# Attention and dense layers on one core: two interleaved streams in a hand-set order, x kept in SBUF, DMA transposes, head pairs on array tiles

## The chip, the cores and the metric

The kernel runs on one core of a Trainium2 chip. The metric is device time in microseconds (us) of that core. Executions of the kernel before spread over 2%.

Engines are named as in the profile: PE is TensorE's matmul, PEld its weight load, DVE VectorE, ACT ScalarE, POOL GpSimd, SP SyncE (here only an issuer of DMAs).

## The reference

Eight batches of twelve heads, 448 tokens, 64 features per head; then two dense layers over the 8 x 448 = 3584 tokens. Cut to what matters:

```python
q_n = q / (norm(q) + 1e-06);  k_n = k / (norm(k) + 1e-06)
attn = softmax(q_n @ k_n.T / tau)             # tau = 0.1
x = (attn @ v)  ->  [3584 tokens, 12 * 64 = 768]
h = x @ w_in                                  # 768 -> 2048
out = maximum(0.01 * h, h) @ w_out            # 2048 -> 768
```

## The kernel before

Batches of attention and chunks of 512 tokens of dense work are written one after the other, and a tile scheduler interleaves them. Per head:

```python
# weights are loaded first, then q, k, v of each batch; rows of 64 f32 = 256 bytes
nc.gpsimd.dma_start(out=w_in_sb, in_=w_in_r);  nc.gpsimd.dma_start(out=w_out_sb, in_=w_out_r)
...
for h in range(H):
    for t in range(NK):                       # 4 tiles of 112 tokens
        nc.vector.tensor_scalar_mul(out=q_hn[:, t, :], in0=q_bf[:, h, t, :],
                                    scalar1=qni[:, h, t : t + 1])
    for t in range(NK):                       # 8 PE transposes into PSUM
        nc.tensor.matmul(out=pqk[:, 0, t, :], lhsT=q_hn[:, t, :], rhs=id128[:PK, :PK], is_transpose=True, ...)
        nc.tensor.matmul(out=pqk[:, 1, t, :], lhsT=k_bf[:, h, t, :], rhs=id128[:PK, :PK], is_transpose=True, ...)
    nc.vector.tensor_copy(out=qkT, in_=pqk)
    for ki in range(NK):
        nc.tensor.matmul(out=sc, lhsT=kT[:, ki, :], rhs=qTf, start=True, stop=True)
        nc.scalar.activation(out=pe[:, ki, :], in_=sc, func=Exp, scale=kni[:, h, ki : ki + 1])
    for ki in range(NK):                      # a 65th column of ones in v gives the sums
        nc.tensor.matmul(out=po, lhsT=v_bf[:PK, h, ki, :], rhs=pe[:, ki, :], ...)
    nc.vector.reciprocal(rsi, po[D : D + 1, :])              # 1 x 448
    nc.gpsimd.partition_broadcast(out_ap=rsb, in_ap=rsi)
    nc.vector.tensor_mul(obf, po[:D, :], rsb)
    nc.sync.dma_start(out=xT[h * D : (h + 1) * D, b * S : (b + 1) * S], in_=obf)   # x to DRAM
```

A dense chunk loads its 512 columns of x back from DRAM, does 16 x 6 matmuls of 512 columns with a leaky ReLU on ACT, and 4 x 2 x 16 matmuls of 512 or 256 columns with a copy on ACT.

## Time and profile before

| before | value |
|---|---|
| time, median of the first 3 runs | 810.55 us (807.48 to 821.59) |
| first matmul | 52.4 us |
| 52 to 240 us: weighing matmuls (attn @ v) done, of 384 | 100, that is 25 of 96 heads |
| granted clock in most of that stretch | 0.50 to 0.59 |
| PE busy from 440 us on | 91 to 99% per stretch of 40 us |

The page's first part (busy time per engine) and three rows of its second (the span in 40 slices of 20.3 us, a digit being tenths):

```profile
PE 664.0 (82%) x3054; PEld 281.4 (35%) x3104; DVE 543.4 (67%) x714; ACT 375.0 (46%) x616; POOL 126.0 (16%) x128
PE   0036775977479988899889999799999999999996
PEclk9999655555559979999598999899999999999999
DMA  9999009305980099009190099207970012001201
```

There are three stages in these digits. For two slices PE does nothing while the DMA engines are full. Then PE is partly busy at half clock. From the middle on it is nearly always busy at full clock.

The costliest groups (line, engine, operation, tiles, shapes, count | busy us, mean ns | idle before, and what ended it):

```profile
L132 ACT ACTIVATE pe<-sc,kni 112x448 bf16<-112x448 f32 x384 | 243.0, 633 | 236.9 <-PE sc L129 235.7
L144 DVE RECIPROCAL rsi<-po 1x448 f32<-1x448 f32 x96 | 282.8, 2949 | 98.7 <-PE po L139 97.8
L112 PE MATMUL tp<-id_58,q_hn 112*64 112x112 bf16 x384 | 66.6, 243 | 68.6 <-DVE q_hn L106 66.3
```

The reciprocal works on one row and costs 2.95 us per head. PE's waits, longest first (total us, times, longest):

```profile
PE tp L112 <- DVE q_hn L106: 66.3, 3, 52.4
PE sc L129 <- ACT pe L132: 31.0, 56, 2.7
```

The 52.4 us are the start. How matmuls follow one another is read from the timeline by differences of starts, since a matmul's end is modelled (start, us, what):

```profile
651.73 0.39 PE L129 MATMUL sc<-qkT 64*112 64x448 bf16 x1
652.05 0.38 PE L139 MATMUL po<-pe,v_bf 112*65 112x448 bf16 x1
652.26 0.81 PE L191 MATMUL po_4942<-w_out_sb,hT 128*128 128x512 bf16 x3
```

A score matmul of 448 columns occupies the array for 0.32 us here, a weighing one for 0.21.

### The profile page before, as it was taken

The numbers are of one execution on the slowest core, as the hardware profiler recorded it, in microseconds if no ns is written. First come the engines' busy times: TensorE is split into PE (matmuls) and PEld (weight loads), VectorE is DVE, ScalarE is ACT, GpSimd is POOL, SyncE is SP. The second block draws the span as 40 slices with busy tenths as digits, with TensorE's granted clock in tenths as the row PEclk, the third lists the DMA queues.
The fourth block names the chain that finished last, engine by engine and source line by source line (L and its number), as shares of the span: only waits on it lengthen the run. The fifth ranks groups of instructions, "written<-read, shape, count | busy, mean of one in ns | idle before, by whom it ended". The sixth has DMA issues, their size and how long they took to land.

```text
span 811.7 us, 8243 instructions
## 1 busy us (share of the span) xinstructions
PE 664.0 (82%) x3054; PEld 281.4 (35%) x3104; DVE 543.4 (67%) x714; ACT 375.0 (46%) x616; POOL 126.0 (16%) x128
## 2 busy tenths in 40 slices
PE   0036775977479988899889999799999999999996
PEld 0012321322123334333343335333443344334543
DVE  0087877767867877689486887789978874775000
ACT  0034434433436653566436664566465643663231
POOL 3120113112301131013110132012201110111000
PEclk9999655555559979999598999899999999999999
DMA  9999009305980099009190099207970012001201
GB/s 172 192 126 29 12 10 99 17 11 44 57 58 12 10 96 104 37 13 68 35 118 25 9 74 88 80 9 55 80 112 12 9 36 96 13 9 36 93 19 59
DMA packets 149496, 45.36 MB, mean 56 GB/s; under 512 B 131536, under 2 KB 145104, under 8 KB 149456
## 3 DMA queue, kind: packets, MB, share of 16 engines
q0 software_dynamic: 132256, 22.81, 53.7%
q1 hardware_dynamic: 17200, 22.03, 8.8%
q8 instruction: 24, 0.39, 0.2%
q14 instruction: 16, 0.13, 0.1%
HBM read 51.12 MB, written 16.52 MB: 83 GB/s over the span
## 4 chain that ended last, share of the span: by engine, by line
PE 64%; ACT 9%; issue 9%; DVE 8%; DMA 7%; POOL 2%; another core or an unknown queue 1%; POOLq 0%; ACTq 0%; SPq 0%; DVEq 0%
PE pm L166 19%; PE sc L129 16%; PE po L139 12%; ACT pe L132 5%; PE tp L112 4%; DMA k_bf<-in_k_dram 4%; PE tp L117 3%; DVE rsi L144 2%; DMA xTc<-xT_bridge 2%; DMA xT_bridge<-obf 1%; DVE q_hn L106 1%; ACT L94 1%; DVE kni L88 1%; DVE qni L88 1%; ACT osb L197 1%
## 5 line engine op out<-in xcount | busy, mean ns | idle before, releaser
L132 ACT ACTIVATE pe<-sc,kni 112x448 bf16<-112x448 f32 x384 | 243.0, 633 | 236.9 <-PE sc L129 235.7
L144 DVE RECIPROCAL rsi<-po 1x448 f32<-1x448 f32 x96 | 282.8, 2949 | 98.7 <-PE po L139 97.8
L129 PE MATMUL sc<-qkT 64*112 64x448 bf16 x384 | 171.4, 446 | 41.7 <-ACT pe L132 31.0
L166 PE MATMUL pm<-xTc,w_in_sb 128*128 128x512 bf16 x641 | 181.4, 388 | 7.5 <-DMA xTc<-xT_bridge 4.1
L139 PE MATMUL po<-pe,v_bf 112*65 112x448 bf16 x384 | 157.1, 431 | 9.3 <-ACT pe L132 8.7
L146 POOL PARTITION_BROADCAST rsb<-rsi x96 | 75.4, 787 | 525.1 <-DVE rsi L144 474.2
L112 PE MATMUL tp<-id_58,q_hn 112*64 112x112 bf16 x384 | 66.6, 243 | 68.6 <-DVE q_hn L106 66.3
L191 PEld LDWEIGHTS <-hT 128*128 128x128 bf16 x896 | 87.1, 101 | 81.1 <-issue 31.6
L129 PEld LDWEIGHTS <-qkT 64*112 64x112 bf16 x384 | 51.3, 136 | 167.4 <-issue 148.8
L166 PEld LDWEIGHTS <-w_in_sb 128*128 128x128 bf16 x672 | 64.2, 103 | 56.9 <-issue 11.0
L112 PEld LDWEIGHTS <-q_hn 112*64 112x64 bf16 x384 | 43.1, 122 | 109.2 <-DVE q_hn L106 71.1
L173 ACT ACTIVATE hT<-pm 128x512 bf16<-128x512 f32 x112 | 66.6, 594 | 25.4 <-PE pm L166 23.1
L139 PEld LDWEIGHTS <-v_bf 112*65 112x65 bf16 x384 | 43.6, 120 | 100.3 <-issue 85.8
L106 DVE TENSOR_SCALAR q_hn<-q_bf,qni 112x64 bf16<-112x64 bf16 x384 | 70.9, 268 | 10.0 <-PE tp L112 6.1
L122 DVE COPY qkT<-tp 64x896 bf16<-64x896 bf16 x96 | 59.1, 615 | 25.3 <-PE tp L117 23.4
L148 DVE TENSOR_TENSOR obf<-po,rsb 64x448 bf16<-64x448 f32 x96 | 58.9, 616 | 21.0 <-POOL rsb L146 20.0
L117 PE MATMUL tp<-id_58,k_bf 112*64 112x112 bf16 x384 | 66.1, 239 | 0.0
L117 PEld LDWEIGHTS <-k_bf 112*64 112x64 bf16 x384 | 45.6, 125 | 11.2 <-issue 11.1
L87 DVE TENSOR_TENSOR norm_sq<-q_bf 112x3072 bf16<-112x3072 bf16 x8 | 14.3, 1786 | 42.2 <-DMA q_bf<-in_q_dram 38.9
L88 DVE TENSOR_REDUCE qni<-norm_sq 112x48 f32<-112x3072 bf16 x8 | 26.6, 3329 | 2.8 <-issue 2.8
L88 DVE TENSOR_REDUCE kni<-norm_sq 112x48 f32<-112x3072 bf16 x8 | 26.7, 3341 | 0.2
L77 POOL DMA_DIRECT2D v_bf<-in_v_dram x8 | 16.0, 1999 | 61.8 <-PE po L139 29.6
(133 smaller groups left out, 297.2 us busy)
## 6 DMA issues: line engine op xcount, KB each, us to landing
out_dram<-osb SPq DMA_DIRECT2D x28, 384.0 KB, 2.3
q_bf<-in_q_dram POOLq DMA_DIRECT2D x8, 672.0 KB, 8.7
k_bf<-in_k_dram POOLq DMA_DIRECT2D x8, 672.0 KB, 9.9
v_bf<-in_v_dram POOLq DMA_DIRECT2D x8, 672.0 KB, 11.0
xT_bridge<-obf SPq DMA_DIRECT2D x96, 56.0 KB, 1.9
xTc<-xT_bridge SPq DMA_DIRECT2D x7, 768.0 KB, 5.0
w_in_sb<-in_moe_w_in_dram POOLq DMA_DIRECT2D x1, 3072.0 KB, 18.6
w_out_sb<-in_moe_w_out_dram POOLq DMA_DIRECT2D x1, 3072.0 KB, 21.9
```

The source lines that it names most:

```text
L88: nc.vector.tensor_reduce(ni_tile, sq, axis=mybir.AxisListType.X, op=mybir.AluOpType.add)
L106: nc.vector.tensor_scalar_mul(out=q_hn[:, t, :], in0=q_bf[:, h, t, :], scalar1=qni[:, h, t : t + 1],)
L112: nc.tensor.matmul(out=pqk[:, 0, t, :], lhsT=q_hn[:, t, :], rhs=id128[:PK, :PK], is_transpose=True, start=(t == 0), stop=False,)
L117: nc.tensor.matmul(out=pqk[:, 1, t, :], lhsT=k_bf[:, h, t, :], rhs=id128[:PK, :PK], is_transpose=True, start=False, stop=(t == NK - 1),)
L129: nc.tensor.matmul(out=sc, lhsT=kT[:, ki, :], rhs=qTf, start=True, stop=True,)
L132: nc.scalar.activation(out=pe[:, ki, :], in_=sc, func=mybir.ActivationFunctionType.Exp, scale=kni[:, h, ki : ki + 1],)
L139: nc.tensor.matmul(out=po, lhsT=v_bf[:PK, h, ki, :], rhs=pe[:, ki, :], start=(ki == 0), stop=(ki == NK - 1),)
L144: nc.vector.reciprocal(rsi, po[D : D + 1, :])
L146: nc.gpsimd.partition_broadcast(out_ap=rsb, in_ap=rsi)
L166: nc.tensor.matmul(out=pm, lhsT=w_in_sb[:, kt, m * 128 : (m + 1) * 128], rhs=xTc[:, kt, :], start=(kt == 0), stop=(kt == KT_DM - 1),)
L173: nc.scalar.activation(out=hT[:, m, :], in_=pm, func=mybir.ActivationFunctionType.Prelu, alpha=0.01,)
L191: nc.tensor.matmul(out=po2[:, :osz], lhsT=hT[:, m, ts * PT : (ts + 1) * PT], rhs=w_out_sb[:, m, ofs : ofs + osz], start=(m == 0), stop=(m ...
```

## The change

The intent: pair the heads, so that two matmuls of 64 rows (row tiles) or 64 columns (column tiles) lie side by side on the array; take the transposes, the DRAM round trip of x and half the reciprocals off the engines; and give PE an instruction order in which dense matmuls fill the time in which attention waits. The new file is a rewrite. Its core, with cuts marked:

```diff
-    q_r = q.rearrange("b h (t p) d -> b h p t d", p=PK)          # 256-byte rows
+    view = "b h (p t) d -> b p h t d"                            # rows of 4 tokens: 1 KB
+    ctx.enter_context(tc.manual_schedule())                      # program order on each engine
+    nc.scalar.preload_act_table_set("natural_log_exp_and_others")
 ...
+    def turn(b, what):                                           # 16 DMA transposes in all
+        nc.sync.dma_start_transpose(out=xt[...], in_=xn.rearrange("p t h d -> p (t h d)"))
-            nc.tensor.matmul(... is_transpose=True ...)          # 768 of them
-            nc.vector.tensor_copy(out=qkT, in_=pqk)
 ...
+    def scores(b, p, half):                                      # two heads on row tiles
+        for ki in (2 * half, 2 * half + 1):
+            for a in range(2):
+                r = slice(64 * a, 64 * a + 64)
+                nc.tensor.matmul(out=sc[:, a, :S], lhsT=kT[r, o : o + 128], rhs=q4[r, :, p, :], ...)
+            nc.scalar.activation(out=pe[:, ki], in_=sc[:PK, :, :S], func=ACTF.Exp, scale=inv_tau)
+    def weigh(b, p):                                             # two heads on column tiles
+        for dst, ones_ in ((sm, True), (po, False)):
+            for ki in range(NT):
+                for a in range(2):
+                    nc.tensor.matmul(out=dst[64 * a : 64 * a + 64, :],
+                        lhsT=ones[:PK, :] if ones_ else vb[:, 2 * p + a, ki, :],
+                        rhs=pe[:, ki, a, :], start=(ki == 0), stop=(ki == NT - 1))
+        nc.vector.reciprocal(rs, sm)                             # 128 x 448, once per pair
+        nc.vector.tensor_mul(st["x", b][:, p, :], po, rs)        # x stays in SBUF
-            nc.gpsimd.partition_broadcast(out_ap=rsb, in_ap=rsi)
-            nc.sync.dma_start(out=xT[...], in_=obf)
 ...
+    def fill(us):                                  # dense work, on an estimated clock
+        end = clock[0] + us
+        while at[0] < len(dense) and clock[0] < end:
+            work, took, b = dense[at[0]]           # layer 1: 1.13 us, layer 2: 2.6 us
+            if done.get(b, 1e9) + 6.0 > clock[0]:  # x of batch b not there yet
+                break
+            work(); clock[0] += took; at[0] += 1
 ...
+    for what in "qkv":
+        load(0, what)
+    nc.gpsimd.dma_start(out=w_in_sb, ...);  nc.gpsimd.dma_start(out=w_out_sb, ...)
+    ... norms, scaling and transposes of batch 0 ...
+    for what in "qkv":
+        load(1, what)
+    for b in range(B):
+        for p in range(HP):                        # 6 head pairs
+            for half in range(2):
+                scores(b, p, half)
+                if half == 1: weigh(the pair before)
+                prepare(b + 1, 2 * p + half)       # norms, scaling, transposes, loads, by step
+                fill(3.0)
```

A half-pair is the work of one call of `scores`: a head pair against two of the four key tiles. `prepare` spreads the next batch over the half-pairs: sums of q at step 0, root of q and sums of k at step 1, root of k at step 2, scaling on POOL from step 3, transposes at steps 4 and 5, the loads after next at steps 6 and 11.

## The prediction

> **What bounds it now.** Three stages. (1) Start: by the waits view PE's first matmul comes at 52.4 us; the two weight loads were issued ahead of q and k, and the loads' 256-byte rows keep the DMA 90% busy to 40 us. (2) About 52 to 240 us: little or no dense work, granted clock 0.50 (stretch table), PE about 75% busy at that clock, and the chain alternates score matmul, 0.64 us exp, 2.95 us reciprocal, broadcast. (3) From about 440 to 812 us PE is 91 to 99% busy per stretch at clock 0.91 to 1.0: PE-bound. Page: PE 664, DVE 543, ACT 375, POOL 126 us of 812.
>
> **Removed.** 768 PE transposes (started 0.05 us apart warm: about 38 us of PE), 96 PSUM copies (59 us DVE), 384 small scalings (71 us DVE), half of the reciprocals (96 to 48 of 2.95 us: 141 us DVE), 75 us of broadcasts, about 40 us of ACT table loads, the DRAM round trip of x, and three quarters of the q/k/v packets (rows become 1 KB).
>
> **Added.** A ones-matmul for the sums; 16 DMA transposes of 688 KB; scaling on POOL (84 calls, about 1.2 us each, estimate); mode changes on the array: in the trace a 448-column score matmul between full-array ones takes 0.32 us start to start, against 0.19 to 0.21.
>
> **Costs after (estimates from those spacings: 448 columns 0.19 us, 384 columns 0.16).** Dense: 768 x 0.19 + 896 x 0.16 = 290 us, cannot shrink. Scores: 384 matmuls in row-tile pairs, 192 x 0.19 = 37. Sums and values: 768 in column-tile pairs, 384 x 0.19 = 73; unpaired it would be 146. The Trainium skill, "TensorE: Matmul & The Clock Gate", Part 3, reports concurrent tiles at 3.07x for four; no run here shows pairs yet. Mode changes, about 0.2 us each around 96 score and 48 weighing groups: 30. PE total about 430. ACT: exp of 896 columns about 0.91 us x 192 = 175, Prelu 69, copies 27, norms 9: 280. DVE: 142 + 30 + 82 + 11 = 265. So PE binds wherever dense work is interleaved, ACT or DVE elsewhere.
>
> **Time by stage (order of the built kernel).** Start until the first score matmul: 33 us (loads, two norms at 5.1 us, scaling, transposes beside the weight load). The first 19 half-pairs have no dense work, at half clock, about 2.65 us each: 50. Then 59 half-pairs hold 235 us of dense work plus 1.45 us of attention each: 320. Another 18 in batches 3, 5, 7 have none, limited by DVE (10 us of norm sums there) and ACT: 45. After the last attention: 17 us of batch 6 and 39 of batch 7, plus hand-over and last store: 60. Sum 508; imperfect pairing and stalls add about 20: **528 us**, ratio about 0.65. Range **485 to 600**. Chances: faster 0.98, same 0.01, slower 0.01.
>
> **What would show it.** Two score matmuls of a pair starting within 0.05 us, and 16 weighing matmuls in 1.5 to 2.0 us (not 3.0). First matmul at 28 to 40 us. One ACT table load. Exp about 0.91 us. Clock near 0.5 for the first 80 to 90 us and about 1.0 in the dense stretches. Weights, x and transposes never topping PE's waits after the start. A dense-only tail near 56 us. POOL under half busy.
>
> **What would make it wrong.** Column-tile matmuls with different moving operands not overlapping (+70 us). Slow weight loads on column tiles. DMA transposes much slower than 10 us each, above all beside the weight load at the start (+10 to 20). The clock halving again in the attention-only stretches of batches 3, 5, 7 (+10 to 30). POOL's scaling several times dearer than estimated, so that a batch waits for its transposes.

## The result, and the profile after

The changed kernel takes 555.61 us (median of 4 runs, 554.02 to 557.2), against 809.01 us before (4 runs of the same rounds, 804.96 to 821.59). The ratio is 0.689, 95% interval 0.685 to 0.693. A ratio here is the mean time of one kernel's runs over that of the other's of the same rounds, so it is not quite the ratio of the medians. Executions over 1.5% slower than the fastest of the same kernel are left out of the means.

The same lines of the page, after (slices of 13.8 us now):

```profile
PE 446.2 (81%) x2816; PEld 216.5 (39%) x2816; DVE 265.8 (48%) x163; ACT 260.0 (47%) x409; POOL 118.3 (21%) x131
PE   0000285589999999499999996799999997999996
PEclk9999999789999999679999999799999999999999
DMA  9999829448149423392449025290560110002013
```

PE now starts in the fifth slice, at 62.7 us, and from the ninth on the row has three dips, in the 17th, the 25th and 26th, and the 34th. The groups that answer those of before:

```profile
L135 ACT ACTIVATE pe<-sc 112x896 bf16<-112x896 f32 x192 | 163.2, 918 | 60.9 <-PE sc L131 60.9
L153 DVE RECIPROCAL rs<-sm 128x448 f32<-128x448 f32 x48 | 141.8, 2953 | 180.9 <-PE sm L146 180.9
L103 POOL TENSOR_TENSOR q_n<-q_bf,q_ni 112x512 bf16<-112x512 bf16 x42 | 42.3, 1038 | 80.9 <-DVE q_ni L99 80.9
```

A reciprocal of 128 rows costs what one of 1 row did (2.953 against 2.949 us), so halving the count halved the cost. PE's waits:

```profile
PE sc L131 <- DMA kT<-k_n: 64.6, 2, 62.7
PE sc L131 <- ACT pe L135: 37.7, 46, 5.4
```

The first matmul waits 62.7 us, and for the k transpose. SP's timeline shows the transposes of batches 0 to 2 (start, time during which SP was issuing it, what):

```profile
24.98 10.41 SPq L114 DMA_TRANSPOSE qT<-q_n  x1
35.45 18.77 SPq L114 DMA_TRANSPOSE kT<-k_n  x1
74.64 3.36 SPq L114 DMA_TRANSPOSE qT<-q_n  x1
81.43 3.74 SPq L114 DMA_TRANSPOSE kT<-k_n  x1
113.94 3.21 SPq L114 DMA_TRANSPOSE qT<-q_n  x1
```

The first two take three to six times as long to issue as the later ones. And the pairs, in a dense stretch of the same timeline:

```profile
159.34 0.55 PE L131 MATMUL sc<-qT,kT 64*128 64x448 bf16 x4
159.83 0.95 PE L146 MATMUL sm<-pe,ones 112*64 112x448 bf16 x8
160.61 0.92 PE L146 MATMUL po<-pe,v_bf 112*64 112x448 bf16 x8
```

Four score matmuls occupy 0.49 us, eight weighing ones 0.78: one 448-column matmul per 0.12 and 0.10 us, where it was 0.32 and 0.21. The single records show the pairs: the score matmuls start at 159.344 and 159.348 us, then at 159.544 and 159.548, and the weighing ones too in twos, 3 to 4 ns apart.

The dips, as stretches (the columns are the length, and each engine's busy time in it; only rows of interest):

```profile
120.00:217.00 97.00, 97.00 (x628) 48.14 (x626) 47.33 (x29) 53.29 (x86) 16.85 (x20) 1.00 0.52 83
217.00:239.00 22.00, 13.56 (x75) 4.94 (x74) 18.24 (x13) 11.02 (x17) 14.08 (x17) 0.66 0.46 77
338.00:358.00 20.00, 11.18 (x75) 4.32 (x73) 17.34 (x13) 11.00 (x17) 12.10 (x14) 0.83 0.51 84
456.00:469.00 13.00, 9.03 (x77) 3.96 (x76) 11.23 (x7) 10.15 (x13) 0.00 (x0) 1.00 0.09 27
```

Where dense work is interleaved (120 to 217 us) PE is busy all the time. In batches 3, 5 and 7 there is a stretch without it, in which DVE, at 83 to 87%, is the busiest engine, and the granted clock falls in two of the three.

Where the time came from, by stage, in the two profiled executions (spans of 811.7 and 553.5 us, 258 apart; the medians are 253 apart):

| stage | before | after |
|---|---|---|
| to the first matmul | 52.4 us | 62.7 us |
| attention with next to no dense work | 52 to 240: 188 us for 25 heads (7.5 each) | 62.7 to 119: 56 us for 19 heads (3.0 each) |
| the rest, mostly PE-bound | 572 us | 434 us |

So the start lost 10 us, and the two other stages gave 132 and 138 us. They don't hold the same share of the work before and after, which is why the second row has the time per head too.

### The profile page after: what moved, and what is told of

Same layout as the page of the kernel before. It is cut to its first block, busy times and chain, and to the rows that moved or that the text cites. A ratio compares the mean times of both kernels' runs of the same rounds, so it can differ in the third digit from the quotient of the medians.

```text
span 553.5 us, 6672 instructions
## 1 busy us (share of the span) xinstructions
PE 446.2 (81%) x2816; PEld 216.5 (39%) x2816; DVE 265.8 (48%) x163; ACT 260.0 (47%) x409; POOL 118.3 (21%) x131
## 4 chain that ended last, share of the span: by engine, by line
PE 73%; DVE 9%; DMA 8%; ACT 5%; SPq 2%; POOL 1%; issue 1%; ACTq 0%; DVEq 0%; POOLq 0%
PE mm L164 27%; PE mm L180 27%; PE sm L146 7%; DMA kT<-k_n 7%; PE sc L131 6%; PE po L146 6%; ACT pe L135 5%; DVE k_ni L87 2%; DVE rs L153 2%; SPq L114 2%; DMA q_bf<-in_q_dram 1%; DVE k_n L86 1%; DVE q_ni L87 1%; POOL k_n L103 1%; DVE q_n L86 1%
## 5 line engine op out<-in xcount | busy, mean ns | idle before, releaser
L153 DVE RECIPROCAL rs<-sm 128x448 f32<-128x448 f32 x48 | 141.8, 2953 | 180.9 <-PE sm L146 180.9
L135 ACT ACTIVATE pe<-sc 112x896 bf16<-112x896 f32 x192 | 163.2, 918 | 60.9 <-PE sc L131 60.9
L164 PE MATMUL mm<-xT,w_in_sb 128*128 128x448 bf16 x768 | 153.9, 355 | 0.0
L180 PE MATMUL mm<-w_out_sb,hT 128*128 128x384 bf16 x896 | 150.1, 326 | 0.0
L131 PE MATMUL sc<-qT,kT 64*128 64x448 bf16 x384 | 62.7, 383 | 102.4 <-DMA kT<-k_n 64.6
L168 ACT ACTIVATE hT<-mm 128x448 bf16<-128x448 f32 x128 | 69.8, 545 | 76.4 <-PE mm L164 76.4
L103 POOL TENSOR_TENSOR q_n<-q_bf,q_ni 112x512 bf16<-112x512 bf16 x42 | 42.3, 1038 | 80.9 <-DVE q_ni L99 80.9
L103 POOL TENSOR_TENSOR k_n<-k_bf,k_ni 112x512 bf16<-112x512 bf16 (+1 forms) x43 | 50.6, 1209 | 22.8 <-DVE k_ni L99 22.8
L146 PE MATMUL sm<-pe,ones 112*64 112x448 bf16 x384 | 51.5, 395 | 0.2 <-DVE rs L153 0.2
L146 PE MATMUL po<-pe,v_bf 112*64 112x448 bf16 x384 | 50.0, 387 | 0.0
## 6 DMA issues: line engine op xcount, KB each, us to landing
w_in_sb<-in_moe_w_in_dram POOLq DMA_DIRECT2D x1, 3072.0 KB, 26.3
```

Of the source, the lines that this page charges most:

```text
L103: eng.tensor_tensor(out=xn[:, :, h0:h1, :].rearrange("p t h d -> p h t d"), in0=x[:, h0:h1], in1=ni[:, h0:h1].unsqueeze(3).to_broadcast([P ...
L131: nc.tensor.matmul(out=sc[:, a, :S], lhsT=kT[r, o : o + 128], rhs=q4[r, :, p, :], start=True, stop=True,)
L135: nc.scalar.activation(out=pe[:, ki], in_=sc[:PK, :, :S], func=ACTF.Exp, scale=inv_tau)
L146: nc.tensor.matmul(out=dst[64 * a : 64 * a + 64, :], lhsT=ones[:PK, :] if ones_ else vb[:, 2 * p + a, ki, :], rhs=pe[:, ki, a, :], start=( ...
L153: nc.vector.reciprocal(rs, sm)
L164: nc.tensor.matmul(out=pm[:, :S], lhsT=w_in_sb[:, kt, m * 128 : (m + 1) * 128], rhs=xT[:, kt, :], start=(kt == 0), stop=(kt == KT - 1),)
```

## The experiments

Two questions were open. Which parts of the change earn the time? And why is it 28 us more than the 528 us forecast, when the forecast's costs per instruction were met? The theory for the second: the first transposes share the DMA engines with 12.6 MB of weights (the f32 bytes read), and the attention-only stretches are held up by DVE's norm sums. The rivals: the first transposes are slow by themselves; and ScalarE's order, not DVE, makes the stretches slow.

All edits are to the changed kernel. Times are medians of 4 runs (e14: 6):

| run | time, us | ratio to before |
|---|---|---|
| changed kernel | 555.6 | 0.689 |
| e1 weights after the first transposes | 555.1 | 0.688 |
| e2 batch 1's loads after them too | 554.9 | 0.688 |
| e3 loops of the weighing swapped | 556.5 | 0.690 |
| e4 root of k later | 556.5 | 0.691 |
| e3b full-array weighing (wrong result) | 612.2 | 0.759 |
| e5 scheduler's order | 555.6 | 0.689 |
| e6 dense work spread | 526.9 | 0.653 |
| e9 weights in gaps | 559.7 | 0.693 |
| e12 loads reordered | 535.3 | 0.662 |
| e14 e12 and e6 together | 506.1 | 0.626 |
| e8 x through DRAM | 555.2 | 0.688 |
| e15 full-array scores (wrong result) | 566.9 | 0.702 |

The changed kernel wasn't run again in the rounds of the experiments, and the rounds used different chips in part. Differences of a few us from its 555.6 are therefore not read as gains or losses.

### Do the pairs earn it? e3, e3b, e15

e3 was meant to take the column pairs apart by order alone:

```diff
-            for ki in range(NT):
-                for a in range(2):
+            for a in range(2):
+                for ki in range(NT):
                     nc.tensor.matmul(out=dst[64 * a : 64 * a + 64, :], ...
```

> The changed kernel with the two loops of the weighing swapped: the four key tiles of one head run one after the other, then those of the other head, so that neighbouring matmuls share a column tile. Same matmuls, same data, same number. Theory (neighbouring matmuls on different column tiles run at the same time): eight of them take about 1.5 us in place of 0.78, PE gains 48 x 1.5 = 72 us of work, of which the dense stretches (37 of 48 pairs) show all: time 600 to 630 us. Rival (the array would overlap them anyway, or the pairs are not what makes them quick): 550 to 565 us.

It measured 556.5 us: nothing. The trace shows that the experiment missed its aim, for the weighing is as fast as before:

```profile
163.29 0.96 PE L146 MATMUL sm<-pe,ones 112*64 112x448 bf16 x8
164.08 0.95 PE L146 MATMUL po<-pe,v_bf 112*64 112x448 bf16 x8
```

Within the eight of the sums, single records still start in twos, 13 ns apart, about every 190 ns. The program as written has four matmuls in a row on one column tile. The records don't name the tile, and they don't show whether the built program kept that order, so that the second four overtook the first is an inference. For the time, the order among the eight made no difference here.

e3b takes the pairs away for real. The result is wrong:

```diff
-  out=dst[64 * a : 64 * a + 64, :], lhsT=ones[:PK, :64] or vb[:, 2 * p + a, ki, :]       # 64 columns
+  out=dst,                          lhsT=ones[:PK, :128] or 128 columns of vb            # 128 columns
```

> A wrong result on purpose: the 16 weighing matmuls of a head pair keep their number, moving operands and columns, but each uses 128 weight columns and writes all 128 rows of sums or values, so that no two can sit side by side on the array. Since the swap of loops changed nothing (two matmuls still started 13 ns apart every 189 ns, although program order put four on one column tile in a row), this is the real removal of the pairs. If the pairs halve the weighing: eight matmuls in 1.5 us instead of 0.78, 48 x 1.45 = 70 us more PE work, time 605 to 630 us. If they do not, 550 to 562 us.

```profile
172.93 0.55 PE L131 MATMUL sc<-qT,kT 64*128 64x448 bf16 x4
173.41 1.69 PE L146 MATMUL sm<-pe,ones 112*128 112x448 bf16 x8
174.93 1.30 PE L146 MATMUL po<-pe,v_bf 112*128 112x448 bf16 x6
```

Eight matmuls now occupy 1.52 us instead of 0.78, and the time is 612.2 us. The column pairs are worth 56.6 us.

e15 does the same to the scores: `lhsT=kT[:, ...]` and `rhs=q4[:, ...]` over all 128 rows.

> A wrong result on purpose: the score matmuls keep their number and columns, but each uses all 128 rows (both heads of the pair at once), so that no two can run side by side on row tiles. If the row pairs halve the scores as the column pairs halved the weighing: four matmuls in about 0.8 us instead of 0.48, 96 groups x 0.35 = 33 us more PE work, a part of it hidden in the attention-only stretches, so 575 to 592 us. If the row pairs earn nothing (their saving lost in changing the array's mode around each group): 550 to 562 us.

```profile
165.99 0.92 PE L131 MATMUL sc<-qT,kT 128*128 128x448 bf16 x4
166.74 3.57 PE L164 MATMUL mm<-xT,w_in_sb 128*128 128x448 bf16 x18
```

A group of four takes 0.75 us, not 0.8, against 0.49 paired. Time 566.9 us: 11.3 us more, between what the two expectations named. The saving is 0.26 us a group, less than half of 0.75; that a paired group changes the array's mode and a full-array one in a dense stretch does not would account for it (see the list below), but no run isolates it. Over the roughly 59 groups in dense stretches that would be 15 us. A part of it came back: in this run batch 0's weighing reached full pace by 69.8 us, in the changed kernel only by 80.5 (the first record of a granted clock begins at 67.6 and 77.4 us). A busier PE getting its clock sooner would fit this, but wasn't tested.

### Does the order, or x in SBUF, earn it? e5, e8

e5 deletes one line, `ctx.enter_context(tc.manual_schedule())`, and lets the scheduler reorder.

> The changed kernel with the hand-set order given up: the line that keeps program order on each engine is removed and the tile scheduler may reorder. In the built program the order of the dense stretches is the same, but the attention-only stretches differ: single layer-1 matmuls and copies are pulled in among the scores. If the hand-set order carries part of the gain: 565 to 590 us. If the structure carries it and not the order: 548 to 562 us.

555.6 us: the hand-set order, beyond the order in which the program is written, earns nothing that these runs can show. The waits move (PE waits for exp 12.6 us instead of 37.7, but 14.4 us for DVE's multiply and 7.1 for ScalarE's copy), and the time stays.

e8 sends x through DRAM again:

```diff
-        nc.vector.tensor_mul(st["x", b][:, p, :], po, rs)
+        nc.vector.tensor_mul(xo, po, rs)
+        nc.sync.dma_start(out=xTd[p * 128 : (p + 1) * 128, b * S : (b + 1) * S], in_=xo)
+        if p == HP - 1:  nc.sync.dma_start(out=st["x", b], in_=xTd[:, batch b] ...)
```

> One part of the change undone: x goes to DRAM by one 448-column write per head pair and comes back by one load per batch, as before the change. In the changed kernel batch 0's x is complete at 102.1 us and first used at 119.0 us, so 17 us of slack against about 7 us for the write (1.9 us) and the load (5.0 us) measured in the kernel before. If the round trip lies within the slack: 552 to 562 us, x in SBUF earns nothing by itself. If it is on the chain: 575 to 620 us, with PE waiting for the load of x once per batch.

555.2 us. The round trip lies within the slack that the order of the dense work leaves; keeping x in SBUF earns nothing measurable here.

### The start: e1, e2, e9, e12

e1 holds the weights back. A copy of two columns that reads the landed transpose and writes into the weight tile makes the load wait, without a race:

```diff
-    nc.gpsimd.dma_start(out=w_in_sb, ...); nc.gpsimd.dma_start(out=w_out_sb, ...)    # before batch 0's norms
 ... norms, transposes of batch 0, load(1, ...)
+    nc.gpsimd.tensor_copy(out=w_in_sb[:, 0, 0:2], in_=st["kT", 0][:, 0:2])
+    nc.gpsimd.dma_start(out=w_in_sb, ...); nc.gpsimd.dma_start(out=w_out_sb, ...)
```

> The changed kernel, but the two weight loads are issued only after the first k transpose has landed (a two-column copy that reads that transpose's result and writes into the weight tile goes ahead of the load); the loads of batch 1 stay where they are. Theory A (the first two transposes take 10.4 us of issue and 27.2 us to landing because they share the 16 DMA engines with 12.6 MB of weights): first score matmul at 38 to 46 us instead of 62.7, time 530 to 540 us. Rival B (the first transposes are slow by themselves, for instance because they are the first): first score matmul stays at 58 to 64 us, time stays 550 to 560 us. Rival C (the start shrinks, but the weights then come too late for the first dense work): first matmul early, and a wait for the weights of 5 us or more appears before the first layer-1 matmul.

e2 moves the copy above batch 1's loads as well.

> As the run before, and the q, k and v loads of batch 1 are held back as well, so that nothing else is loading while q and k of batch 0 are transposed. Theory A: both transposes at their undisturbed pace (about 5 us from issue to landing), first score matmul at 35 to 38 us, 3 to 8 us earlier than in the run before; time 525 to 537 us. If the loads of batch 1 do not matter, the first matmul is where it was in the run before. If holding them back makes batch 1's transposes late, a wait for the transpose of 3 us or more appears at the start of batch 1.

Both confirm the mechanism and neither gains: 555.1 and 554.9 us. PE's longest wait in e1:

```profile
PE sc L131 <- DMA kT<-k_n: 62.0, 2, 39.6
```

The 62.0 us are two waits, of 39.6 us for batch 0's transpose and of 22.4 for batch 1's. SP's timeline in e1 has both pairs of transposes:

```profile
24.86 3.38 SPq L114 DMA_TRANSPOSE qT<-q_n  x1
30.05 3.81 SPq L114 DMA_TRANSPOSE kT<-k_n  x1
57.00 16.31 SPq L114 DMA_TRANSPOSE qT<-q_n  x1
73.40 12.90 SPq L114 DMA_TRANSPOSE kT<-k_n  x1
```

Without the weights beside them, batch 0's transposes are issued as quickly as any, so they are not slow by being the first. The first matmul came at 39.6 us, with batch 1's loads beside the k transpose, and at 35.2 us in e2, with nothing beside it. But now batch 1's transposes meet the weights and take 16.3 and 12.9 us to issue. Batch 1's first score came at 92.9 and 95.1 us, where it had been 92.5. What was gained at the first batch was paid at the second.

The DMA packets say why. A transpose is 2688 packets of 256 bytes, 168 on each of 16 engines. Alone, one takes 18 ns (median). The layer-2 weights come in packets of 1536 bytes at 134 ns, q and k in packets of 512 bytes at 60 ns. The Trainium skill, "DMA: Bandwidth & Descriptors", section "Queues, rings and completion order", states that each DMA engine goes round-robin between its queues, a packet at a time (a packet in the page's sense can hold several of the rows that the profile counts as packets). If each transpose packet waits for one of the others, the estimate is 168 x 134 ns = 22.5 us beside the weights, and 168 x (60 + 18) ns = 13 us beside q and k. Measured from issue to landing: 26.3 us for the changed kernel's first q transpose, whose packets ran beside the weights nearly all the way, 11.0 us for its second k transpose, beside the loads of q and k for the most part, and 5.1 us alone (e2). The first k transpose took 27.2 us because it stood behind the q transpose in its queue: it landed 11.4 us after it, with batch 1's loads beside it. The sizes fit, and the packet records of the trace show the alternation, one for one in number: from 36.0 to 47.2 us 1257 packets of transposes and 1254 of the layer-2 weights started, from 54 to 60 us 1442 of transposes and 1425 of batch 1's loads.

e9 puts the layer-1 weights after batch 1's loads, and the layer-2 weights after batch 1's k transpose.

> Runs e1 and e2 moved the first matmul to 39.6 and 35.2 us, but batch 1's k transpose then landed at 92.9 and 95.1 us (92.5 before): it had met the weights instead. Here the layer-1 weights go out after batch 0's transposes and batch 1's loads, and the layer-2 weights only after batch 1's k transpose has landed. Theory F (one 256-byte transpose packet waits for a large weight packet at each turn, so a transpose must have the queue engines to itself): first matmul at 34 to 37 us, batch 1's first score at 69 to 76 us, time 528 to 540 us. Rival G (the volume of loads alone sets when batch 1 can start): batch 1's first score at 85 us or later, time above 545 us.

Both of batch 1's transposes ran nearly alone (6.9 and 6.6 us from issue to landing) and the second landed at 72.6 us, as theory F has it. Yet the time was 559.7 us, for the gain went a third way:

```profile
95.79 1.76 DVE L86 TENSOR_TENSOR q_n<-q_bf 112x3072 bf16<-112x3072 bf16 x1 [19.59 <-DMA q_bf<-in_q_dram]
102.44 0.56 PE L131 MATMUL sc<-qT,kT 64*128 64x448 bf16 x2 [24.55 <-ACT pe L135]
```

Batch 2's q load had queued behind the layer-2 weights and landed at 95.8 us. The root of its sums stands in ScalarE's program order ahead of batch 1's exps, so the exps waited for a load that they don't need. The waits view blames "ACT pe" for 24.6 us; the cause is a DMA two steps back.

e12 keeps e9's place for the layer-1 weights, issues batch 2's q and k loads ahead of the layer-2 weights, and takes up batch 2's preparation four half-pairs later (cut):

```diff
+        if b == 2:
+            step -= 4
 ...
         elif step == 6 and b + 1 < B:
+            if b == 1: nc.gpsimd.tensor_copy(out=w_out_sb[:, 0, 0:2], in_=st["kT", 1][:, 0:2])
             load(b + 1, "q"); load(b + 1, "k")
+            if b == 1: nc.gpsimd.dma_start(out=w_out_sb, ...)
```

> Run e9 brought batch 1's k transpose in at 72.7 us, but batch 2's q load then queued behind the layer-2 weights, landed at 95.8 us, and the root of batch 2's q sums, ahead of the exps in ScalarE's order, held PE for 24.6 us. Here batch 2's q and k loads go ahead of the layer-2 weights, and batch 2's norms, scaling and transposes are taken up four half-pairs later in batch 1. If this chain of late loads is the whole reason why e1, e2 and e9 gained nothing: no wait of PE above 5 us after the first matmul except for batch 1's k transpose (at 72 to 75 us), first layer-1 matmul at 95 to 103 us in place of 119.0, time 530 to 542 us. If the time comes back once more, above 548 us, and the wait that takes it is to be named.

```profile
PE sc L131 <- ACT pe L135: 46.7, 46, 9.9
PE sc L131 <- DMA kT<-k_n: 35.0, 1, 35.0
```

535.3 us, with the first layer-1 matmul at 95.7 us instead of 119.0. The gain of 20 us is kept. One expectation failed: a wait of 9.9 us for exp is left, up to 49.5 us. It is of the kind that e9 showed: batch 1's q, whose load was held back, gets its sums at 48.0 us, and the root of them stands ahead of batch 0's exps.

### The attention-only stretches: e4, e6

e4 moves only the root of k, which stands ahead of the exps in ScalarE's order, from step 2 to step 5 (its inverse, scaling and transpose go with it).

> The changed kernel with the square root of k's sums moved three steps later in ScalarE's order (its inverse, scaling and transpose move with it). Theory (the exps of the next pairs stand behind a root that waits for 8 us of VectorE work, 5.4 us of PE idle in batch 3, 4.1 us in batch 1, the same in batch 5): these waits shrink to under 1.5 us, PE's waits for exp fall from 37.7 us to 20 to 27, time 538 to 550 us. Rival (VectorE itself is the limit there, so that the wait moves to the sums matmul behind the reciprocal): time 551 to 558 us and a new wait of PE for the reciprocal of 8 us or more in sum.

```profile
PE sc L131 <- ACT pe L135: 23.2, 40, 0.9
PE sm L146 <- DVE rs L153: 14.6, 3, 5.0
```

556.5 us. The waits for exp fell from 37.7 to 23.2 us, and 14.6 us of waits for DVE's reciprocal took their place. In batches 3 and 5 a wait of 5.4 us for exp became one of 4.8 us for the reciprocal. (In batch 1 the k transpose, moved with the root, kept PE waiting for 8.2 us where it had been 1.9.) The rival is right: DVE is the limit in these stretches. It has 3.6 us per head pair and another 10.2 us of norm sums at the stretch's beginning.

e6 gives DVE time instead. The dense work is handed out by a running account, so that no stretch is without it:

```diff
     def fill(us):
-        end = clock[0] + us
+        owed[0] += us                       # what a half-pair overshoots is taken off the next
+        end = clock[0] + owed[0]
 ...
-            fill(3.0)
+            fill(3.05)                      # and a third buffer for x
```

In the old form every half-pair got its 3.0 us afresh, so two layer-2 groups (5.2 us) counted as one allotment, and the stock of dense work ran out in every second batch.

> The changed kernel with the dense work handed out by a running account (3.05 us per half-pair, the overshoot carried to the next half-pair) instead of afresh per half-pair, and a third buffer for x. The batches 3, 5 and 7 then have no stretch without dense work. Theory D (in these stretches VectorE's norm sums hold up attention, because no PE work is there to cover them, and the clock halves): PE's waits for exp fall from 37.7 to about 15 us, time 525 to 538 us. Rival E (what is gained there comes back as ScalarE or VectorE waits in the dense stretches): 548 to 558 us.

The row "PE" of e6's page, and PE's longest wait for ScalarE:

```profile
PE   0000186759999999999999999999999999999996
```

```profile
PE sc L131 <- ACT pe L135: 15.7, 25, 4.2
```

526.9 us, 28.7 less, and the dips of the row "PE" are gone. The third buffer for x came with it, and its own share wasn't measured.

### Both together: e14

e14 is e12 with e6's account, and with the margin between a batch's attention and its dense work cut from 6.0 to 3.0 on the kernel's own clock.

> The reordered loads of the run above, the dense work spread by a running account (run e6), and the margin between a batch's attention and its first dense work cut from 6 to 3 on the kernel's own clock. If the two gains are in different places and add up: 526.9 - 20 and a few us for the earlier dense work, 495 to 510 us, PE idle after its first dense matmul below 10 us in sum. If the start's gain is lost again: 520 to 530 us. This is the version meant to beat both kernels.

The row "PE" of e14's page, and PE's two longest waits:

```profile
PE   0011868599989999999999999999899999999996
```

```profile
PE sc L131 <- DMA kT<-k_n: 35.0, 1, 35.0
PE sc L131 <- ACT pe L135: 19.4, 21, 9.8
```

506.1 us (6 runs, 503.78 to 507.96), correct, ratio 0.626 to before. It beats both kernels. The gains of e12 (20.3 us) and e6 (28.7 us) add up to 49.0, and 49.5 came, with the cut of the margin, whose own share was not measured. PE's waits after its first dense matmul, which came at 81.9 us, sum to 8.2 us (7.5 and 0.5 for ScalarE's results of the dense layers, 0.2 for exp), below 10 as expected. The other 19.2 us of waits for exp lie before it, 9.8 of them in the wait that e12 had left.

## Why the prediction was right or wrong

The measured 555.6 us lies in the range of 485 to 600, and the direction was right. The centre was 28 us too low. Stage by stage, in the profiled execution of 553.5 us:

| stage | predicted | measured | how read |
|---|---|---|---|
| start to the first score matmul | 33 us | 62.7 us | PE's waits |
| 19 half-pairs without dense work | 50 us | 56.3 us | 62.7 to 119.0 |
| 59 half-pairs with dense work | 320 us | 319.8 us | 119.0 to 493.0, less the next row |
| 18 half-pairs without, in batches 3, 5, 7 | 45 us | 54.2 us | 21.7 + 19.9 + 12.5, rounded |
| tail | 60 us | 60.5 us | 493.0 to 553.5 |
| imperfect pairing and stalls | 20 us | - | in the rows above |

The stages came out some 45 us above the forecast's sum of 508. The allowance of 20 us, meant for pairing and stalls, made the miss look smaller: the dense stretches took what had been forecast without it. That the centre was off by 28 us and not by 45 is luck.

- **The step that failed is "Start until the first score matmul: 33 us".** It was listed under what would make the prediction wrong (transposes beside the weight load, "+10 to 20"), but the term was sized without it. It measured 62.7 us. e1 and e2 show the reason: with nothing else loading the same chain takes 35.2 us. They also show that the stage couldn't be judged alone: all the loads up to batch 2 share one set of DMA engines, and the gain was kept only once e12 had ordered them all.
- **Pairs on the array: right.** 16 weighing matmuls were to take 1.5 to 2.0 us and took 1.63 (159.83 to 161.46). The Trainium skill, "TensorE: Matmul & The Clock Gate", Part 3, has tiles working at the same time; e3b shows that taking it away costs 56.6 us. The forecast's 70 us, for no overlap, is what PE's work alone would give (48 x 16 x 0.093 = 71 us). The rest may have been hidden where PE isn't the limit: 37 of the 48 pairs lie in dense stretches, and 37 x 16 x 0.093 is 55 us.
- **Mode changes: right in kind, half the size.** The Trainium skill, "TensorEngine Tiling (Array Packing)", section "Key Properties", says that a change of tiling mode drains the array. In e15, without a change, four score matmuls took 0.75 us, four times 0.19; the two pairs of the changed kernel took 0.49 us, 0.11 more than two times 0.19, where about 0.2 was forecast. That these 0.11 us are the drain is not shown by itself.
- **Costs per instruction: right.** Exp 0.918 us (0.91 forecast), POOL scaling 1.04 (1.2), DVE 265.8 us in all (265), one table load. ACT took 260 us (280). The prediction doesn't say what its figures for exp and for POOL were worked out from.
- **The stretches of batches 3, 5 and 7: the mechanism right, the size 9 us too small.** Batches 3 and 5 took 20 to 22 us and batch 7, with no next batch to prepare, 12.5. e4 and e6 confirm that DVE was the limit.
- **Half clock at the start: right in part, and not to be read from the row "PEclk".** That row shows 9 in the fifth and sixth slices (55 to 83 us), while 16 weighing matmuls took 3.1 us at 69 us and 1.6 us at 80 us. The trace's first record of a granted clock begins at 77.4 us, and the row counts time without a record as full speed. From there to 119 us the records have half clock for 13.7 us in sum. With the slow matmuls before 77.4 us, that is about half of the stretch (an estimate), where the forecast had all of it; it took 56.3 us all the same, and not 50.
- **Within the forecast's list of removals, what earned little.** x in SBUF (e8) and the hand-set order (e5) earn nothing measurable.

What stays open: the pairs account for 56.6 us and 11.3 us of the 253 us when taken away one at a time. The rest wasn't split. The DMA transposes with PE's 768 transposes gone, the halved reciprocals, two heads per exp, the single table load and the 1 KB rows changed together, and no run undoes one of them alone. That they brought attention without dense work from 7.5 to 3.0 us per head is measured; how it divides is not.

## What to carry to other kernels

A gain at the start of a pipeline is only kept if the loads that were moved don't meet the next batch's small-packet transfers: order all transfers up to the steady state, and read after each step where the next wait is. Hand out filler work by a running account rather than per slot, or the overshoot of one slot will be missing later, at the very place where another engine needs the cover. Before crediting a part of a rewrite, undo it alone: here array pairs carried 57 us, while the order by hand and x in SBUF carried nothing.

## What the Trainium skill lacked or had wrong

- "DMA: Bandwidth & Descriptors", section "Rules for kernel authors", says that a transpose next to ordinary DMAs needs nothing. For correctness these runs agree. It lacks the price of running beside them: for 688 KB 5.1 us from issue to landing alone, 11.0 us for the most part beside the loads of q and k, 26.3 us beside the weights.
- "TensorE: Matmul & The Clock Gate", Part 3, has matmuls start and end strictly in program order. In e3, where four matmuls in a row use one column tile as the program is written, matmuls still started in twos, 13 ns apart about every 190 ns, and eight took 0.79 us. The trace names neither the tiles nor the order of the built program, so this may count against strict order and doesn't prove that one matmul overtook another.
- No page gives the reciprocal's price on VectorE: 2.95 us for 448 columns, or 6.6 ns a column with all overhead, the same for 1 and for 128 partitions.
